# Keys and values of the last head loaded in two transfers each

## The chip, the cores and the metric

The kernel runs on one core of a Trainium2 chip. The metric is device time in microseconds (us), as the median of several executions; a profiled execution is recorded beside them, and all views below come from it. Within a core there are TensorE (PE, with its weight loads shown apart as PEld), VectorE (DVE), ScalarE (ACT), GpSimd (POOL) and SyncE (SP), and 16 DMA engines that move data between the device memory (HBM) and the core's memory (SBUF, 128 partitions). In this kernel SP issues nearly all DMAs, ACT four small ones at the start.

## The reference

One decode step (batch 1, one token, D = 576): a sigmoid gate mixes the output of an attention over the last W = 4096 cached keys with that of a dense GELU block.

```python
q = (x @ wq).reshape(1, 1, 32, 128).transpose(0, 2, 1, 3)
k = repeat(k_cache[:, :, Sk - W:, :], 2, axis=1)      # 16 key heads, Sk = 32768, W = 4096
v = repeat(v_cache[:, :, Sk - W:, :], 2, axis=1)
p = softmax(einsum("bhqd,bhkd->bhqk", q, k) * 128 ** -0.5)
a = einsum("bhqk,bhkd->bhqd", p, v).transpose(0, 2, 1, 3).reshape(1, 1, 4096) @ wo
b = gelu(x @ w1 + b1) @ w2 + b2                        # F = 4608
g = sigmoid((x * gate_w).sum(-1))
out = g * a + (1 - g) * b
```

Everything is bfloat16 in HBM. One head's keys are 4096 rows of 128 values, 1 MB; so are its values. With 16 heads that is 32 MB, and the four weight matrices are another 20 MB. A softmax followed by a weighted sum does not depend on the order of the keys, as long as keys and values are ordered alike.

## The kernel before

Each head's window of 4096 keys lies in one tile of 128 partitions x 32 chunks x 128 values. `load_k` (L83) and `load_v` (L90) fill it with one DMA: partition p gets the 32 consecutive rows 32p to 32p + 31, which is one run of 8 KB for each partition. `load_flat` (L99) loads pieces of `wq` and `w1` in the same way, one run for each partition (9,216 bytes, the last `w1` piece 4,608). `wo` (L421) has two runs of 4,608 bytes for each partition, `w2` (L431) one run of 10,368 bytes, its last group cut in two pieces of 6,912 and 3,456 bytes.

The instruction order is written by hand (`manual_schedule`, L72). The main loop (L395) runs over `h` from 0 to 20: it issues the keys of head h + 1 and the values of head h - 4, and, at five places, a piece of `w1`; then for each of eight groups of four chunks it transposes keys of head h + 1 on PE (`transposes`, L179: PE to PSUM, then DVE or ACT to SBUF), computes scores of head h (`scores`, L202), and multiplies values of head h - 5 (`values`, L265). Softmax runs for four heads at a time. After the loop SP issues four loads of `wo` and five of `w2` (L418 to L432), the last thing that the kernel reads. PE multiplies the attention output by `wo` (into `a_ps`) and the GELU output by `w2` (into `b_ps`, L496); one DVE instruction (L501) mixes both, and one DMA (L504) writes the output, four rows of 144.

So the order on SP's queue near the change is: values of head 9 and keys of head 15 (h = 14), values of heads 10 to 15, `wo` four times, `w2` five times, output. SP waits before an issue for two things where they apply: for a free buffer (10 for keys and values together, 8 for weights), and for the transfer issued eight places earlier, since the completion semaphores of its DMAs are used in turn, eight in all.

Four small loads go through ACT (L112 to L114): `x9` and `gw9` with 128 rows each, `b1g` with 4 rows of 2,304 bytes, `b2_row` with a single row of 1,152 bytes.

Of the kernel before, what the change touches and what calls it, by code (L numbers as in the profile page):

```python
# [9 lines left out]
BF16 = mybir.dt.bfloat16  # L10
# [6 lines left out]
def kernel(  # L17
# [15 lines left out]
    nc = tc.nc  # L33

    P = 128
    D = 576
    Hq, Hkv, Dh = 32, 16, 128
    Sk, W = 32768, 4096
    NCH = W // P
# [22 lines left out]
    kv_pool = ctx.enter_context(tc.tile_pool(name="kv_pool", bufs=10))  # L62
# [17 lines left out]
    NOG = Hq // OJ  # L80
    wo_view = A_wo.rearrange("(o p j) n -> p o (j n)", p=P, j=OJ)

    def load_k(h):  # L83
        t = kv_pool.tile([P, NCH, Dh], BF16, name="k_t", tag="kv")
        nc.sync.dma_start(  # L85
            out=t[:], in_=A_k_cache[0, h, Sk - W : Sk, :].rearrange("(p c) d -> p c d", p=P)
        )
        return t

    def load_v(h):  # L90
        t = kv_pool.tile([P, NCH, Dh], BF16, name="v_t", tag="kv")
        nc.sync.dma_start(  # L92
            out=t[:], in_=A_v_cache[0, h, Sk - W : Sk, :].rearrange("(p c) d -> p c d", p=P)
        )
        return t

    WMAX = RJ * D

# [15 lines left out]
    nc.scalar.dma_start(out=b2_row[:], in_=B_b2.rearrange("(o n) -> o n", o=1))  # L114

    k_tiles[0] = load_k(0)
    wq_t = []
    QP = NM * QB // 4
    for i in range(4):
        if i == 2:  # L120
            k_tiles[1] = load_k(1)
        wq_t.append(load_flat(wq_flat, i * QP * Dh, QP * Dh, "wq_t"))
# [15 lines left out]
    for o in range(2):  # L138
        nc.vector.tensor_reduce(
            out=par[:, o : o + 1],  # L140
            in_=ident_f[:].rearrange("p (i o) -> p o i", o=2)[:, o, :],
# [7 lines left out]
        out=turn[:].rearrange("p j (h q) -> p j h q", h=OJ),  # L149
        in_=ident[:].rearrange("p (o q j) -> p j o q", o=1, j=OJ).to_broadcast(  # L150
            [P, OJ, OJ, P // OJ]
        ),
# [4 lines left out]
        out=m_r[:], in_=ident_f[:].rearrange("p (s r) -> p r s", r=R), axis=AX.X, op=ALU.add  # L157
# [3 lines left out]
        out=m_hl[:], in_=ident_f[:].rearrange("p (h q) -> p h q", h=OJ), axis=AX.X, op=ALU.add  # L161
# [117 lines left out]
    for i in range(NBL):  # L279
# [5 lines left out]
        out=junk9[:], in0=x9[:], in1=gw9[:], scale=1.0, scalar=0.0,  # L285
# [11 lines left out]
        out=omg[:], in0=g_t[:], scalar1=-1.0, scalar2=1.0, op0=ALU.mult, op1=ALU.add  # L297
# [3 lines left out]
    for b in range(NM * QB):  # L301
# [3 lines left out]
        m, c = b // QB, b % QB  # L305
# [12 lines left out]
    for g in (1, 3):  # L318
        for hl in range(HB):
            lo = R * g + 2 * hl  # L320
            nc.vector.tensor_copy(  # L321
                out=qz[:, hl::HB, lo : lo + 2],
                in_=q_ps[:].rearrange("p o (b r) -> p (o b) r", r=R)[:, :, 2 * hl : 2 * hl + 2],
# [71 lines left out]
    for h in range(Hkv + LAG):  # L395
        if 1 <= h < Hkv - 1:
            k_tiles[h + 1] = load_k(h + 1)
        if 0 <= h - HB < Hkv:
            v_tiles[h - HB] = load_v(h - HB)
        w1_next = (W1_AT[h], w1_load(W1_AT[h])) if h in W1_AT else None  # L400
        for i in range(NBL):
            if 1 <= h < Hkv - 1:
                transposes(h + 1, i)
            if i in (2, 5) and h < Hkv:
                scores(h, i // 3)
            if i in (0, 1, 3, 6) and chain:
                chain.pop(0)()
            if h >= LAG:
                values(h - LAG, i)
        if w1_ready is not None:  # L410
            w1_mul(*w1_ready)
            if w1_ready[0] == len(PIECES) - 1:
                gelu()
        w1_ready = w1_next
        if h % HB == HB - 1 and h < Hkv:
            chain = softmax(h // HB)

    wo_t = []  # L418
    for i in range(NOG // 2):
        t = w_pool.tile([P, WMAX], BF16, name="wo_t", tag="w")  # L420
        nc.sync.dma_start(  # L421
            out=t[:, 0 : 2 * OJ * D].rearrange("p (o n) -> p o n", o=2),
            in_=wo_view[:, 2 * i : 2 * i + 2, :],
# [3 lines left out]
    for g in range(NG):  # L427
        t = w_pool.tile([P, WMAX], BF16, name="w2_t", tag="w")
# [8 lines left out]
        out=sg[:],  # L437
# [14 lines left out]
    for j in range(OJ):  # L452
# [3 lines left out]
        out=ow_m[:],  # L456
# [6 lines left out]
        out=ow_f[:].rearrange("p j o -> p (j o)"), in_=ow_m[:], axis=AX.X, op=ALU.add  # L463
# [17 lines left out]
    for o in range(NOG):  # L481
# [8 lines left out]
        out=a_sb[:], in0=a_ps[:], scalar1=g_t[:, 0:1], scalar2=None, op0=ALU.mult  # L490
# [5 lines left out]
    for g in range(NG):  # L496
# [5 lines left out]
        out=y[:], in0=b_ps[:], scalar=omg[:, 0:1], in1=a_sb[:], op0=ALU.mult, op1=ALU.add  # L502
    )
    nc.sync.dma_start(  # L504
        out=out.rearrange("a b (t n) -> (a b t) n", t=NQ), in_=y[0 : 32 * (NQ - 1) + 1 : 32, :]
# [31 lines left out]
```

## Time and profile before

| what | value |
|---|---|
| median of 3 executions | 138.4 us (138.38 to 138.7) |
| profiled execution, its time | 138.9 us |
| profiled execution, its span | 137.1 us |
| bytes moved by DMA | 53.88 MB in 8035 packets |
| PE, PEld, DVE, ACT busy | 75%, 61%, 42%, 31% of the span |
| granted TensorE clock, mean | 0.755 |
| transfer of 1 MB of keys, issue to landing | 20.0 us |

The span runs from the first to the last instruction; times on it are counted from its start. The execution's own time is 1.8 us longer than the span, for what lies around it. A DMA's "landing" is the moment at which all its parts have been reported complete. The trace also holds a record of every DMA packet (queue, bytes, start, duration), without the number of the engine that moved it, and of every increment of a semaphore.

### The profile page before, as it was taken

To read this page: it belongs to the slowest core of one execution; us is meant where nothing else is said; L and a number is where in the kernel's file an instruction comes from. 1 tells how busy PE (TensorE), PEld (TensorE's weight loads), DVE (VectorE), ACT (ScalarE), POOL (GpSimd) and SP (SyncE) were. 2 spreads that over 40 slices of the span, in tenths; PEclk is the share of its full clock that TensorE was granted. 3 is DMA by queue.
4 is the path that set the end of the run, shared out by engine and by line. 5 is a ranking of instruction groups with operands and counts; after the bars stand their busy time and mean duration, and the time that the engine had idled before them with its cause. 6 is when DMAs were issued, how large, how long until landed. Compare 5 with 4: busy or idle time off the path is not lost.

```text
span 137.1 us, 3928 instructions
## 1 busy us (share of the span) xinstructions
PE 103.5 (75%) x1779; PEld 83.4 (61%) x1779; DVE 57.4 (42%) x127; ACT 42.1 (31%) x75; POOL 1.4 (1%) x7
## 2 busy tenths in 40 slices
PE   0377765999969999988999986999795966343361
PEld 0357753768847977776877964788564855233350
DVE  5171431464477257735566367275723121010001
ACT  0351330355356246633356261554322000000000
POOL 4000000000000000000000000000000000000000
PEclk9999997579779779997589996589655555555555
DMA  4899999999999999999999999999999999999820
GB/s 153 350 418 422 423 427 426 425 427 428 421 421 421 422 415 418 418 418 423 426 419 416 423 415 417 421 413 421 421 421 419 417 418 421 432 430 421 359 105 8
DMA packets 8035, 53.88 MB, mean 393 GB/s; under 512 B 1101, under 2 KB 1102, under 8 KB 2514
## 3 DMA queue, kind: packets, MB, share of 16 engines
q1 hardware_dynamic: 7720, 53.61, 94.0%
q8 instruction: 14, 0.23, 0.7%
q10 hardware_dynamic: 298, 0.02, 0.1%
q14 instruction: 3, 0.02, 0.1%
HBM read 53.62 MB, written 0.00 MB: 391 GB/s over the span
## 4 chain that ended last, share of the span: by engine, by line
DMA 95%; SPq 1%; ACTq 0%; PE 0%; issue 0%; DVE 0%
DMA w_t<-in_B_w_dram 30%; DMA k_t<-in_A_k_cache_dram 29%; DMA wo_t<-in_A_wo_dram 16%; DMA v_t<-in_A_v_cache_dram 14%; DMA gw<-in_gate_w_dram 7%; SPq L85 1%; ACTq L112 0%; PE b_ps L471 0%; SPq L101 0%; DVE y L501 0%; SPq L92 0%
## 5 line engine op out<-in xcount | busy, mean ns | idle before, releaser
L184 PE MATMUL tp<-ident,k_t 128*128 128x128 bf16 x512 | 53.3, 255 | 10.0 <-DMA k_t<-in_A_k_cache_dram 8.2
L193 DVE CAST kT<-tp 128x512 bf16<-128x512 f32 x64 | 43.4, 689 | 33.8 <-PE tp L184 32.1
L195 ACT CAST kT<-tp 128x512 bf16<-128x512 f32 x64 | 37.5, 586 | 54.7 <-PE tp L184 54.3
L184 PEld LDWEIGHTS <-k_t 128*128 128x128 bf16 x512 | 38.0, 113 | 14.9 <-DMA k_t<-in_A_k_cache_dram 9.6
L270 PEld LDWEIGHTS <-v_t 128*128 128x128 bf16 x512 | 23.5, 105 | 7.3 <-issue 7.1
L270 PE MATMUL o_ps<-et,v_t 128*128 128x2 bf16 x512 | 26.8, 167 | 0.3 <-DVE et L259 0.3
L210 PE MATMUL s_ps<-kT,qz 128*32 128x512 bf16 x128 | 15.6, 486 | 0.7 <-DVE qz L321 0.7
L354 PE MATMUL h_ps<-x,w_t 128*128 128x2 bf16 x162 | 10.4, 199 | 0.0
L354 PEld LDWEIGHTS <-w_t 128*128 128x128 bf16 x162 | 10.1, 158 | 0.0
L471 PE MATMUL b_ps<-w_t,gt 128*1 128x144 bf16 x144 | 5.2, 320 | 5.7 <-DMA w_t<-in_B_w_dram 5.7
L471 PE MATMUL a_ps<-wo_t,ow 128*1 128x144 bf16 x128 | 4.5, 320 | 5.1 <-DMA wo_t<-in_A_wo_dram 4.0
L471 PEld LDWEIGHTS <-gt 128*1 128x1 bf16 x144 | 4.1, 115 | 6.7 <-issue 6.6
L471 PEld LDWEIGHTS <-ow 128*1 128x1 bf16 x128 | 3.6, 116 | 5.8 <-issue 4.6
L210 PEld LDWEIGHTS <-qz 128*32 128x32 bf16 x128 | 3.3, 96 | 4.6 <-issue 2.5
L307 PE MATMUL q_ps<-x,wq_t 128*128 128x2 bf16 x144 | 4.3, 166 | 2.2 <-DMA wq_t<-in_A_wq_dram 2.2
L307 PEld LDWEIGHTS <-wq_t 128*128 128x128 bf16 x144 | 4.2, 102 | 2.5 <-DMA wq_t<-in_A_wq_dram 2.5
L501 DVE SCALAR_TENSOR_TENSOR y<-b_ps,omg,a_sb 128x144 bf16<-128x144 f32 x1 | 0.4, 366 | 11.3 <-PE b_ps L471 11.3
L247 ACT ACTIVATE pr<-s_ps,nb 128x512 bf16<-128x512 f32 x4 | 2.7, 687 | 4.2 <-DVE nb L244 3.9
L489 DVE TENSOR_SCALAR a_sb<-a_ps,g_t 128x144 f32<-128x144 f32 x1 | 0.4, 367 | 8.6 <-PE a_ps L471 8.6
L232 PE MATMUL mT<-ident_f,mx 128*1 128x128 f32 x4 | 1.3, 321 | 3.4 <-DVE mx L228 3.4
L228 DVE TENSOR_REDUCE mx<-s_ps 128x1 f32<-128x512 f32 x4 | 2.7, 682 | 1.7 <-PE s_ps L210 1.7
L255 PE MATMUL pT<-ident,pr 128*128 128x128 bf16 x16 | 2.3, 289 | 0.7 <-ACT pr L247 0.7
(59 smaller groups left out, 26.8 us busy)
## 6 DMA issues: line engine op xcount, KB each, us to landing
k_t<-in_A_k_cache_dram SPq DMA_DIRECT2D x16, 1024.0 KB, 20.0
v_t<-in_A_v_cache_dram SPq DMA_DIRECT2D x16, 1024.0 KB, 20.3
wq_t<-in_A_wq_dram SPq DMA_DIRECT2D x4, 1152.0 KB, 12.4
w_t<-in_B_w_dram SPq DMA_DIRECT2D x4, 1152.0 KB, 20.4
wo_t<-in_A_wo_dram SPq DMA_DIRECT2D x4, 1152.0 KB, 21.0
w_t<-in_B_w_dram SPq DMA_DIRECT2D x3, 1296.0 KB, 21.2
w_t<-in_B_w_dram SPq DMA_DIRECT2D x1, 864.0 KB
w_t<-in_B_w_dram SPq DMA_DIRECT2D x1, 576.0 KB
```

The source lines that it names most:

```text
L85: nc.sync.dma_start(out=t[:], in_=A_k_cache[0, h, Sk - W : Sk, :].rearrange("(p c) d -> p c d", p=P))
L184: nc.tensor.matmul(tp[:, c * P : (c + 1) * P], lhsT=k_tiles[h][:, i * BC + c, :], rhs=ident[:], start=True, stop=True,)
L193: nc.vector.tensor_copy(out=dst, in_=tp[:])
L195: nc.scalar.copy(out=dst, in_=tp[:])
L210: nc.tensor.matmul(s_tiles[b][32 * t : 32 * (t + 1), :], lhsT=qz[:, h, lo : lo + 32], rhs=kT[h][:, i * BC * P : (i + 1) * BC * P], start=( ...
L228: nc.vector.tensor_reduce(out=mx[:], in_=s_ps[:], axis=AX.X, op=ALU.max)
L247: nc.scalar.activation(out=pr[:], in_=s_ps[:], func=ACT.Exp, bias=nb[:, 0:1], scale=SCALE, accum_out=sums[:, b : b + 1],)
L255: nc.tensor.transpose(out=pT[:, c, :], in_=pr[:, c * P : (c + 1) * P], identity=ident[:])
L270: nc.tensor.matmul(o_ps[:, 2 * h : 2 * h + 2], lhsT=v_tiles[h][:, i * BC + c, :], rhs=ets[b][:, c, col : col + 2], start=(i == 0 and c == ...
L307: nc.tensor.matmul(q_ps[:, :, c], lhsT=wq_t[b // QP][:, off : off + Dh], rhs=x2[:, m, :], start=(b == 0), stop=(m == NM - 1), skip_group_c ...
L354: nc.tensor.matmul(h_ps[:, j, gl::GH], lhsT=t[:, off : off + U - RJ + 1 : RJ], rhs=x2[:, m, :], start=False, stop=(m == NM - 1), skip_grou ...
L471: nc.tensor.matmul(acc[32 * t : 32 * t + 1, :], lhsT=col, rhs=rows[:, t * DQ : (t + 1) * DQ], start=start, stop=stop,)
```

## The change

`load_k` and `load_v` call a common `load_kv`. For heads 0 to 14 it issues the same DMA as before. For head 15 it issues two. The first fills chunks 0 to 23 of each partition from the first 3,072 rows of the window (partition p gets rows 24p to 24p + 23, a run of 6,144 bytes). The second fills chunks 24 to 31 from the last 1,024 rows, cut into 128 blocks of eight rows (2,048 bytes). Its source is written with three dimensions: 8 rows, 16 blocks in each, 2,048 bytes in a block; block number 8b + a goes to partition 16a + b. The destination is 128 partitions of 2,048 bytes. Which key sits in which partition and chunk changes for head 15, in the same way for keys and values.

```diff
+    CE = 8
+
+    def load_kv(cache, h, name):
+        t = kv_pool.tile([P, NCH, Dh], BF16, name=name, tag="kv")
+        src = cache[0, h, Sk - W : Sk, :]
+        if h < Hkv - 1:
+            nc.sync.dma_start(out=t[:], in_=src.rearrange("(p c) d -> p c d", p=P))
+            return t
+
+        CA = NCH - CE
+        nc.sync.dma_start(
+            out=t[:, 0:CA, :], in_=src[0 : P * CA, :].rearrange("(p c) d -> p c d", p=P)
+        )
+        nc.sync.dma_start(
+            out=t[:, CA:NCH, :],
+            in_=src[P * CA : W, :].rearrange("(b a c) d -> a b (c d)", a=8, b=P // 8),
+        )
+        return t
+
     def load_k(h):
-        t = kv_pool.tile([P, NCH, Dh], BF16, name="k_t", tag="kv")
-        nc.sync.dma_start(
-            out=t[:], in_=A_k_cache[0, h, Sk - W : Sk, :].rearrange("(p c) d -> p c d", p=P)
-        )
-        return t
+        return load_kv(A_k_cache, h, "k_t")
 
     def load_v(h):
-        t = kv_pool.tile([P, NCH, Dh], BF16, name="v_t", tag="kv")
-        nc.sync.dma_start(
-            out=t[:], in_=A_v_cache[0, h, Sk - W : Sk, :].rearrange("(p c) d -> p c d", p=P)
-        )
-        return t
+        return load_kv(A_v_cache, h, "v_t")
```

PE, DVE, ACT and POOL execute the same instructions in the same order as before; SP has two more DMA issues.

More of the change, by code (lines that the diff above doesn't have):

```diff
@@ L81, with load_k @@
     wo_view = A_wo.rearrange("(o p j) n -> p o (j n)", p=P, j=OJ)
-    def load_k(h):
-        t = kv_pool.tile([P, NCH, Dh], BF16, name="k_t", tag="kv")
-        nc.sync.dma_start(
-            out=t[:], in_=A_k_cache[0, h, Sk - W : Sk, :].rearrange("(p c) d -> p c d", p=P)
-        )
-        return t
+    CE = 8
[6 more added lines that the diff above has]
+        CA = NCH - CE
+        nc.sync.dma_start(
+            out=t[:, 0:CA, :], in_=src[0 : P * CA, :].rearrange("(p c) d -> p c d", p=P)
[3 more added lines that the diff above has]
+            in_=src[P * CA : W, :].rearrange("(b a c) d -> a b (c d)", a=8, b=P // 8),
+        )
+        return t
+    def load_k(h):
+        return load_kv(A_k_cache, h, "k_t")
     def load_v(h):
-        t = kv_pool.tile([P, NCH, Dh], BF16, name="v_t", tag="kv")
-        nc.sync.dma_start(
-            out=t[:], in_=A_v_cache[0, h, Sk - W : Sk, :].rearrange("(p c) d -> p c d", p=P)
-        )
-        return t
+        return load_kv(A_v_cache, h, "v_t")
     WMAX = RJ * D
```

## The prediction

> **What bounds the kernel now.** I read the chain of waits first. By engine it is nearly all DMA, and in order of time (start, us, what) it ends with a load of `w2`:
>
> ```profile
> DMA 95%; SPq 1%; ACTq 0%; PE 0%; issue 0%; DVE 0%
> ```
> ```profile
> 112.74 20.78 DMA w_t<-in_B_w_dram
> 133.52 0.04 issue
> 133.56 0.56 PE b_ps L471 x11
> 134.12 0.02 issue
> 134.15 0.37 DVE y L501
> ```
>
> The last transfer lands at 133.52; 3.6 us of matmuls, mix and output follow whatever came before. So the time is 133.52 plus a fixed tail, and only an earlier last landing helps. Next, the DMA rows of the page (40 slices of 3.43 us) and the DMA view of the stretch 126.0 to 137.1 alone (40 slices of 0.28 us):
>
> ```profile
> DMA  4899999999999999999999999999999999999820
> GB/s 153 350 418 422 423 427 426 425 427 428 421 421 421 422 415 418 418 418 423 426 419 416 423 415 417 421 413 421 421 421 419 417 418 421 432 430 421 359 105 8
> ```
> ```profile
> DMA  9998998999687665543322210000200000000100
> ```
>
> The 16 DMA engines run full from the second slice on at about 420 GB/s, yet they do not stop together: from 129 us on the busy share falls step by step until 133. Engines run out of work one after the other, and the last one sets the end.
>
> Why are they uneven? Every big load gives each engine the same bytes. The page's queues and the semaphore records tell:
>
> ```profile
> q1 hardware_dynamic: 7720, 53.61, 94.0%
> q8 instruction: 14, 0.23, 0.7%
> ```
>
> Queue 8 fetches instructions, 14 packets of 16 KB. On one engine a packet's record starts 4 ns before the previous one ends, within 1 ns nearly throughout, so the packet records can be chained into 16 engines. The chains show that the 14 fetches go round eight engines in turn and never touch the other eight. A fetch sets its engine back by about 1.5 us (a fetch at 90.9: the spread of one transfer's 16 increments was 2.60 us before it and 4.15 after). The last `w2` piece's 16 increments, from the semaphore records, on the span's scale:
>
> ```
> eight engines without a fetch: 129.35 129.37 129.54 129.72 130.14 130.44 130.47 130.69
> one fetch each:                131.49 131.51 131.91
> two fetches each:              132.60 132.75 133.11 133.24 133.52
> ```
>
> The two groups do not overlap. Call them early and late: the early group is done 2.83 us before the end (133.52 - 130.69).
>
> **The change part by part.** *How many engines the second transfer uses.* The semaphore records show an increment for each engine that took part: 16 for the loads with 128 rows, 4 for `b1g` with 4 rows, 1 for `b2_row` with one (both beside one more from the issuer, for the rest). A source of 8 rows onto 128 partitions is not in this trace; between 8 and 16 engines I take 8, since the rows cannot be dealt to 16 without cutting them. *Which eight.* Following the four `b1g` packets (from 8.84 to 9.13 us) along their chains, three end on early engines for certain; the fourth, which also carried `b2_row`, meets another chain at the same nanosecond at 15.7 us, and of the two continuations one is early and the other late (its small irregularities go on in the early one). So small row counts seem to use the same engines, nested, none of them where the fetches go; I take the eight to be the early group.
>
> [...]
>
> *Price of bytes.* Packet records by size, median: 4,608 bytes 178 ns, 8,192 bytes 309 ns. That is 131 ns for 3,584 bytes, so 2,048 bytes are worth 74.9 ns and a packet has 9.6 ns of its own, of which 4 overlap.
>
> *First transfers.* On each engine 8 packets of 8,192 become 8 of 6,144 bytes: 8 x 74.9 = 0.60 us less for each of keys and values, 1.20 us in all on every engine. For the late group that is the whole change: its last engine ends at 133.52 - 1.20 = 132.32.
>
> *Second transfers.* 128 blocks over 8 engines are 16 packets of 2,048 bytes each. No row has that size. By the line above a packet takes 84.5 - 4 = 80.5 ns from start to start; the nearest rows give bounds: `b2_row`'s 1,152 bytes took 73 ns (69 net), `b1g`'s 2,304 bytes 93 ns (89 net). I take 80.5 and add 5 ns for the completion write: 16 x 80.5 + 5 = 1.29 us, less the 0.60 saved, so +0.69 us for each transfer and +1.39 for both. The early group's last engine ends at 130.69 + 1.39 = 132.08 (bounds 131.71 and 132.35). It stays within 0.03 us of the late group's 132.32 at worst.
>
> *Sum.* The last landing goes from 133.52 to 132.32 (bounds 132.32 to 132.35): -1.20 us. In the profiled execution's own time 138.9 - 1.2 = 137.7; that execution stands 0.5 us above the median of 138.4, so the median becomes 137.2.
>
> *Issues on SP.* Two more, 0.33 us each by the rows of `k_t`, at most the 0.65 us of the output's issue:
>
> ```profile
> 52.18 0.33 SPq L85 DMA_DIRECT2D k_t<-in_A_k_cache_dram  x1
> 54.66 0.33 SPq L92 DMA_DIRECT2D v_t<-in_A_v_cache_dram  x1
> 57.16 0.33 SPq L85 DMA_DIRECT2D k_t<-in_A_k_cache_dram  x1
> ...
> 134.54 0.65 SPq L504 DMA_DIRECT2D out_dram<-y  x1
> ```
>
> Behind them wait the values of heads 10 to 15, `wo` and `w2`. Each issue waits for the transfer eight places before, so one more place delays each of them by about one step of 2.5 us (52.18, 54.66, 57.16). What hides this is the stock of work in the queue: 20.0 us from issue to landing for 1 MB. With two of the eight places filled by 0.75 and 0.25 MB the stock is 7 MB instead of 8, some 17.5 us; even the early engines, which run up to 4.2 us ahead, do not empty it. Cost nothing; without that cover, a step of 2.5 us.
>
> *PE.* The last two of eight groups of head 15 wait for the second transfer. It follows the first in the queue and rides the engines that are ahead, so these groups can wait a little longer for each other, but PE is only half busy from 110 us on (7.95 of 16 us between 110 and 126), and nothing on the path that ends last hangs on it. The order of keys changes in no instruction.
>
> [...] By the trace, 512 KB on eight engines costs these eight time and frees the others of it. [...] Were all engines in step, that would make the end 1.39 us later by the prices above (139.8 us); the falling busy share before the end says that they are not.
>
> **The rivals.**
>
> *A. The eight engines are, or include, the late ones.* For it: only three of four are sure, and nothing shows four of the early eight under a small load. Against: fetches turn over exactly eight engines, and those three are not among them. The carriers pay +1.39 us, so the kernel ends at 133.52 + 1.39 = 134.91: 139.8 us, slower. It decides as soon as any carrier ended after 132.13 before (133.52 - 1.39), which are the five engines with two fetches. [...]
>
> *B. All 16 engines share the second transfer*, split by the 128 partitions. For it: `x9`, whose source has 64 rows, landed by 16. Against: the same count for 64 and 128 says nothing of 8. Each engine then has 8 packets of 8,192 as 16 of 6,144 and 2,048: for both loads 2 x (8 x 5.6 + 5) = 0.10 us more: 138.5 us, no change.
>
> *C. Blocks of 2,048 bytes, 16 KB apart on one engine, are much slower than 89 ns.* For it: no row has such a step, and 1,152 bytes were dear at 73 ns. Against: `b1g`'s 93 ns came at full load. At 110 ns net the early group ends at 130.69 + 2 x (1.76 + 0.005 - 0.60) = 133.02: 137.9 us. From 126 ns on (130.69 + 2.83) it is slower than before.
>
> **How the numbers follow.** Forecast (two groups, eight early carriers) 0.70; A 0.10; B 0.07; C 0.13, of which faster 0.08, no change 0.02, slower 0.03. A change under 0.3%, 0.4 us, cannot be told from none here. Faster 0.70 + 0.08 = 0.78; same 0.07 + 0.02 = 0.09; slower 0.10 + 0.03 = 0.13. The time is the forecast's 137.2. The medians shown differ by up to 0.3 us, which sets the low end, 136.9; upward the range takes in most of C and B, to 138.5, and leaves out A and the dear part of C. The forecast's own range is 136.9 to 137.5.
>
> **What would show it right or wrong.** Right: 256 packets of 2,048 bytes at 80 to 90 ns; 8 increments and one of the issuer for each second transfer; the last `w2` piece's increments within about 2 us of each other instead of 4.2, two groups ending near 132.1 and 132.3; last landing 1.2 us earlier, same 14 fetches. Wrong: 16 increments (B); spread grown to about 6.8 us (A); packets over 100 ns (C); gaps on the DMA engines before 126 us, if the queue's stock did run out.

## The result, and the profile after

The changed kernel is slower: a median of 143.0 us (141.35 to 143.3, four executions) against 138.39 us, a ratio of 1.0305 with a 95% interval of 1.0265 to 1.0345. The profiled execution took 143.3 us, its span is 141.5 us; before it was 138.9 and 137.1. So 4.4 us of span are to be found. Ratios, here and below, compare the means of executions in the fast state; one execution of `e1_near` below, of 142.87 us, is left out of its ratio as a slow one.

The end of the chain of waits, in order of time (start, us, what), is the same as before, only later: the last piece of `w2` lands at 137.91 instead of 133.52, and the tail behind it is unchanged.

```profile
115.52 22.38 DMA w_t<-in_B_w_dram
137.91 0.04 issue
137.95 0.56 PE b_ps L482 x12
138.50 0.02 issue
138.53 0.37 DVE y L512
```

The page's DMA rows of the changed kernel (40 slices of 3.54 us) show where it was lost:

```profile
DMA  4999999999999999999999999999999999999710
GB/s 137 372 405 421 416 423 428 427 423 424 419 421 426 414 419 417 419 424 421 424 419 421 421 406 422 367 289 419 419 417 349 300 414 424 432 430 420 317 58 3
```

There are two dips in GB/s, at 88 to 95 us and at 106 to 113, while the busy digits stay at 9: the DMA engines were not short of work, their packets took longer. These are the stretches in which the two second transfers ran. The view by stretches gives (stretch and its length, busy us of PE, PEld, DVE, ACT, POOL with counts, granted TensorE clock, DMA share, GB/s), first for the kernel before, then for the changed one:

```profile
90.00:96.00 6.00, 5.70 (x112) 4.90 (x108) 3.49 (x10) 3.19 (x7) 0.00 (x0) 0.97 1.01 418
96.00:107.00 11.00, 8.64 (x134) 6.43 (x132) 4.80 (x12) 3.02 (x6) 0.00 (x0) 0.56 1.01 418
107.00:113.00 6.00, 4.58 (x136) 4.23 (x133) 1.29 (x6) 0.00 (x0) 0.00 (x0) 0.50 1.02 416
```
```profile
90.00:96.00 6.00, 6.00 (x112) 5.34 (x110) 3.70 (x6) 2.93 (x5) 0.00 (x0) 0.87 1.04 315
96.00:107.00 11.00, 8.77 (x142) 6.53 (x140) 5.45 (x15) 2.72 (x6) 0.00 (x0) 0.61 1.01 416
107.00:113.00 6.00, 4.15 (x133) 4.01 (x133) 0.52 (x2) 0.52 (x2) 0.00 (x0) 0.50 1.03 309
```

Between the dips the rate is the old one (416 against 418). In the dips it is 315 and 309 instead of 418 and 416: 103/418 x 6 us + 107/416 x 6 us = 3.0 us lost by all 16 engines together.

The packet records say whose packets grew. The 256 packets of 2,048 bytes had a median of 131 ns (the first ones 84). Summed over all packets from 15 us on, the time above each size's undisturbed record, divided by 16 engines and less the same sum before, is 0.71 us for 2,048 bytes, 0.58 for 6,144 (the first transfers), 0.69 for 8,192 (other keys and values) and 1.09 for the 4,608 bytes of `wo`. More than three quarters of the loss fell on packets other than those of the second transfers.

The 16 increments of the last `w2` piece, on the span's scale, summed up:

```
                mean of the 16    last    last - mean
before               131.24      133.52      2.28
changed              134.67      137.91      3.24
```

The mean moved by 3.4 us, about what the dips cost (engines were 0.26 us later in the mean already at 32 us), and the last engine stands another 1.0 us further behind the mean than before. Two questions follow: why the packets were slow, and which engines were loaded.

### The profile page after: what moved, and what is told of

Read it like the earlier page. It is cut to its first block, busy times and chain, and to the rows that moved or that the text cites. A ratio compares the mean times of both kernels' runs of the same rounds, so it can differ in the third digit from the quotient of the medians.

```text
span 141.5 us, 3930 instructions
## 1 busy us (share of the span) xinstructions
PE 102.4 (72%) x1779; PEld 82.9 (59%) x1779; DVE 57.5 (41%) x127; ACT 41.9 (30%) x75; POOL 1.4 (1%) x7
## 4 chain that ended last, share of the span: by engine, by line
DMA 90%; PE 5%; DVE 1%; SPq 1%; ACTq 0%; issue 0%; DVEq 0%
DMA k_t<-in_A_k_cache_dram 40%; DMA w_t<-in_B_w_dram 16%; DMA v_t<-in_A_v_cache_dram 14%; DMA wo_t<-in_A_wo_dram 14%; DMA gw<-in_gate_w_dram 6%; PE tp L195 2%; PE h_ps L365 2%; DVE kT L204 1%; ACTq L123 0%; PE h_ps L353 0%; PE b_ps L482 0%; SPq L112 0%; DVE y L512 0%; SPq L89 0%; PE s_ps L221 0%
## 5 line engine op out<-in xcount | busy, mean ns | idle before, releaser
L281 PEld LDWEIGHTS <-v_t 128*128 128x128 bf16 x512 | 24.0, 106 | 8.5 <-issue 7.3
```

What stands on the lines that cost most here:

```text
L281: nc.tensor.matmul(o_ps[:, 2 * h : 2 * h + 2], lhsT=v_tiles[h][:, i * BC + c, :], rhs=ets[b][:, c, col : col + 2], start=(i == 0 and c == ...
```

## The experiments

Each ratio below is to the kernel before on the same chip, whose median was 138.46 or 138.47 us throughout. The theories are named as in the expectations: S, the step between the blocks in HBM makes them slow; N, eight engines instead of sixteen are the cost; P, the place in SBUF, partitions that other engines write at the same time. No trace here names the engine or the partition of a packet. That one engine carries one row of a source is my reading of the increments (eight for the 8 rows of each second transfer in the changed kernel, four for `b1g` with 4 rows and one for `b2_row` with one row before), which partitions a row fills follows from the kernel's text, and which engines fill them in the 128-row loads is P's assumption.

**The source without its step** (`e1_near`), in the changed kernel:

```diff
-            in_=src[P * CA : W, :].rearrange("(b a c) d -> a b (c d)", a=8, b=P // 8),
+            in_=src[W - 1152 : W, :].rearrange("(a r) d -> a r d", a=8)[:, 0 : P, :].rearrange(
+                "a (b c) d -> a b (c d)", c=CE
+            ),
```

> The second transfer keeps 8 rows of 16 blocks of 2,048 bytes and the same destination, but the 16 blocks of a row are neighbours in HBM (32 KB in one piece) instead of 16 KB apart. It reads 1,024 of the last 1,152 rows of the window, so 128 keys come twice and 128 are left out, and the output differs for that. Theory S (the step in the source makes the blocks slow): packets of 2,048 bytes fall from the changed kernel's 131 ns to 84 to 90 ns, no dip of the DMA rate, time 137.2 to 139.8 us depending on which engines carry them. Theory P (the eight engines write partitions that other engines are writing at the same time): nothing changes, packets about 130 ns, time 141.5 to 143.3 us.

Measured 141.24 us, ratio 1.0187 (1.0147 to 1.0226). The packets kept a median of 128.5 ns, and the two dips are there, 276 and 275 GB/s in the worst of 40 slices of 3.48 us:

```profile
GB/s 134 396 403 428 420 428 423 429 426 424 421 416 423 425 410 423 416 419 417 430 423 414 423 412 423 409 276 385 416 423 402 275 405 422 422 431 420 404 171 3
```

S is out as the cause of the slow packets. The time is 1.8 us below the changed kernel's, though, and just below the 141.5 us that P expected at the least; "Which engines" comes back to it.

**The same cut over 128 rows** (`e2_step`): both transfers take column pieces of the old layout.

```diff
-            out=t[:, 0:CA, :], in_=src[0 : P * CA, :].rearrange("(p c) d -> p c d", p=P)
+            out=t[:, 0:CA, :], in_=src.rearrange("(p c) d -> p c d", p=P)[:, 0:CA, :]
...
-            in_=src[P * CA : W, :].rearrange("(b a c) d -> a b (c d)", a=8, b=P // 8),
+            in_=src.rearrange("(p c) d -> p c d", p=P)[:, CA:NCH, :],
```

> Two transfers each, but the second with 128 source rows of 2,048 bytes (the last eight chunks of each partition's old run, 8 KB apart), so all 16 engines share it as they share every other load. Theory S (small blocks with a step in the source are slow): packets of 2,048 bytes above 100 ns, time 139 to 141 us. Theory P (the place written to): packets 84 to 90 ns, no dip of the rate, 138.4 to 138.7 us. The same 138.4 to 138.7 us from theory N (using eight engines alone is the cost).

Measured 138.65 us, ratio 1.0011 (0.9998 to 1.0024). The 256 packets took 84 to 91 ns (5% to 95%). Splitting the load, two more issues and blocks of 2,048 bytes cost nothing that can be told. The same three stretches of this run have the old rates:

```profile
90.00:96.00 6.00, 6.00 (x112) 5.34 (x111) 3.74 (x7) 2.92 (x5) 0.00 (x0) 0.87 1.02 416
96.00:107.00 11.00, 8.14 (x142) 6.36 (x140) 5.40 (x15) 3.24 (x7) 0.00 (x0) 0.77 1.01 415
107.00:113.00 6.00, 4.79 (x145) 4.51 (x143) 1.25 (x5) 0.00 (x0) 0.00 (x0) 0.50 1.03 418
```

**Four transfers of 32 partitions** in place of the one second transfer (`e3_four`), and **16 rows of 8 blocks** (`e4_rows16`):

```diff
+        for m in range(4):
+            lo = P * CA + 256 * m
+            nc.sync.dma_start(
+                out=t[32 * m : 32 * (m + 1), CA:NCH, :],
+                in_=src[lo : lo + 256, :].rearrange("(b a c) d -> a b (c d)", a=8, b=4),
+            )
```
```diff
-            in_=src[P * CA : W, :].rearrange("(b a c) d -> a b (c d)", a=8, b=P // 8),
+            in_=src[P * CA : W, :].rearrange("(b a c) d -> a b (c d)", a=16, b=P // 16),
```

> The second transfer is cut into four of 32 partitions each, each with a source of 8 rows of 4 blocks 16 KB apart: still eight engines, still 2,048-byte blocks, but engine a now writes partitions 4a to 4a + 3 of the 32. Theory P: the eight engines no longer meet each other, and only two of the four quarters meet another engine's normal partitions; 2,048-byte packets fall in two groups, near 84 to 90 ns and above 110 ns; excess packet time well below the changed kernel's 1.6 us an engine and transfer; 138.5 to 141 us. Theory S or N: all packets stay near 130 ns, 141.5 to 143.5 us.

> The second transfer has a source of 16 rows of 8 blocks (32 KB apart) instead of 8 rows of 16: all 16 engines take part, engine a writing partitions 8a to 8a + 7. Theory N (eight engines alone is the cost): 138.4 to 138.7 us, packets 84 to 90 ns. Theory S (step in the source): packets 120 ns or more. Theory P: packets 100 to 140 ns where engines meet, half as many of them an engine, excess below 0.8 us an engine and transfer, 138.6 to 140.2 us.

`e3_four`: 140.86 us, 1.0178 (1.0155 to 1.02). The packets came in two kinds, as P has it: of the keys' 128 packets in order of time, the first four eighths (the first pair of quarters) have medians of 84, 84, 86 and 106 ns, the last four 166, 133, 102 and 116 ns. The excess fell less than I had said: the dips remain (300 and 274 GB/s).

`e4_rows16`: 141.28 us, 1.0206 (1.0187 to 1.0225), a median of 105 ns, and slower than the 140.2 us that P allowed. All 16 engines took part, the dips are there, and the loss is as large as in `e1_near` with eight:

```profile
90.00:96.00 6.00, 4.88 (x98) 4.04 (x96) 3.98 (x12) 2.75 (x6) 0.00 (x0) 1.00 1.02 337
96.00:107.00 11.00, 9.15 (x152) 6.96 (x152) 4.37 (x10) 2.94 (x6) 0.00 (x0) 0.51 1.01 415
107.00:113.00 6.00, 3.98 (x116) 3.62 (x113) 0.01 (x1) 0.00 (x0) 0.00 (x0) 0.50 1.02 336
```

So N is out as the cause of the dips: what `e2_step` and `e4_rows16` do not share is the shape of the source, and with it, by the reading above, who writes which partition (and the step in HBM, which the next runs settle).

**The place alone.** The kernel before, unchanged, with extra transfers behind the last keys and the last values into a spare tile that nothing reads. `f1_low` is below; `f2_high` differs in one number, the first partition (64 + 32 * m):

```diff
+        if h == Hkv - 1:
+            x = const.tile([P, 8 * Dh], BF16, name="x_" + name)
+            for m in (0, 1):
+                nc.sync.dma_start(
+                    out=x[32 * m : 32 * (m + 1), :],
+                    in_=src[256 * m : 256 * (m + 1), :].rearrange("(b a c) d -> a b (c d)", a=8, b=4),
+                )
```

`f3_eights` sends the same bytes to partitions 0 to 63 in one transfer (a=8, b=8), `f4_stride` 128 rows with the changed kernel's 16 KB step to all partitions:

```diff
...
+                out=x[:],
+                in_=cache[0, h, Sk - 2 * W : Sk, :].rearrange("(p c) d -> p c d", p=P)[:, 0:8, :]
+                .rearrange("p c d -> p (c d)"),
...
```

> The kernel before, whose last keys and values are each followed by two extra transfers of 64 KB into a spare tile that nothing reads: sources of 8 rows of 4 blocks of 2,048 bytes, 16 KB apart, onto partitions 0 to 31 and 32 to 63, so that each of eight engines writes four partitions. Theory P (a transfer is slow where its engines write partitions that other engines write in the normal loads; by the earlier quarters these partitions are the engines' own): 2,048-byte packets 84 to 90 ns, excess packet time below 0.1 us, no dip of the rate; the eight engines get 2 x 8 x 80 ns = 1.3 us more, so 138.4 us if none of them is a late one, up to 139.8 us if one is. Theory S (step or form of the source): packets 100 ns or more, as in the next run.

> As the run with partitions 0 to 63, same sources, bytes, engines and number of transfers, but onto partitions 64 to 95 and 96 to 127. Theory P: these are other engines' partitions; packets 120 ns or more, packets of other transfers beside them lengthened too, excess 0.4 to 0.8 us an engine for each pair, time 139.3 to 141 us. Theory S: no difference from the run before.

> The same extra bytes onto partitions 0 to 63, but in one transfer of 8 rows of 8 blocks, so engine a writes partitions 8a to 8a + 7 instead of four of its own in each half. Theory P: the engines meet each other and each other's normal loads; packets 100 to 140 ns, excess 0.3 to 0.8 us a transfer, 139 to 140.5 us. Theory S: as the run onto partitions 0 to 63 in quarters.

> The kernel before with one extra transfer of 256 KB after the last keys and one after the last values into a spare tile: 128 source rows of 2,048 bytes, 16 KB apart as in the changed kernel, over all 16 engines and their normal partitions. Theory P: packets 84 to 90 ns, excess below 0.1 us, time longer by the bytes alone, 2 x 8 x 80 ns = 1.3 us: 139.7 us. Theory S: packets above 100 ns and 140.3 us or more.

```
run          us      ratio (95%)                2,048-byte packets, 5% / median / 95%, ns
f1_low     139.85   1.0094 (1.0074 to 1.0113)      84 /  84 /  85
f2_high    141.54   1.0218 (1.0195 to 1.0241)      84 / 117 / 177
f3_eights  142.01   1.0223 (1.0162 to 1.0284)      84 / 104 / 160
f4_stride  139.94   1.0107 (1.0081 to 1.0133)      84 /  84 /  88
```

The stretches of `f1_low`, then of `f2_high`:

```profile
90.00:96.00 6.00, 4.47 (x81) 4.06 (x80) 3.83 (x11) 2.09 (x5) 0.00 (x0) 0.83 1.01 415
96.00:107.00 11.00, 9.15 (x142) 6.62 (x140) 3.94 (x10) 3.02 (x6) 0.00 (x0) 0.50 1.01 419
107.00:113.00 6.00, 4.28 (x133) 3.98 (x130) 1.15 (x5) 0.00 (x0) 0.00 (x0) 0.50 1.01 413
```
```profile
90.00:96.00 6.00, 3.07 (x62) 2.66 (x60) 2.97 (x10) 1.99 (x4) 0.00 (x0) 0.83 1.01 325
96.00:107.00 11.00, 9.29 (x151) 7.21 (x151) 4.40 (x9) 3.12 (x6) 0.00 (x0) 0.66 1.02 422
107.00:113.00 6.00, 3.51 (x126) 3.43 (x126) 0.24 (x2) 0.00 (x0) 0.00 (x0) 0.50 1.01 320
```

Same bytes, sources, engine count and number of transfers; moved by 64 partitions, the rate falls from 415 to 325 and from 413 to 320 GB/s. `f4_stride` cost 1.48 us, where its bytes were estimated at 2 x 8 x 80 ns = 1.3 us, and its packets took 84 ns: the 16 KB step did not slow them. Nor are the high partitions slow as such: `e2_step` and `f4_stride` write all 128 at 84 ns, and `f3_eights`, which deals the low 64 out differently, is slow on them. P is shown as far as it goes: the partitions decide (84 ns in `f1_low`, 117 in `f2_high`), and on the same partitions how they are dealt to the rows (104 in `f3_eights`). That the packets are slow where an engine writes partitions that other engines write in the 128-row loads agrees with both, but is my reading; no run shows why. Its sizes were too small: `f2_high` and `f3_eights` are slower than the 141 and 140.5 us that P allowed.

**Which engines.** `f1_low` has no slow packets, so its records can be chained, and the engines that carry 2,048-byte packets stand out: six without a fetch, and two that had two fetches. The last `w2` completions were written by those two, at 133.78 and 133.96, the next engine at 132.97 (starts of packet records; the increments are recorded some 0.45 us later). To see it from the load, longer blocks, and four engines instead of eight:

```diff
-            x = const.tile([P, 8 * Dh], BF16, name="x_" + name)
+            x = const.tile([P, 28 * Dh], BF16, name="x_" + name)
...
-                    in_=src[256 * m : 256 * (m + 1), :].rearrange("(b a c) d -> a b (c d)", a=8, b=4),
+                    in_=src[896 * m : 896 * (m + 1), :].rearrange("(b a c) d -> a b (c d)", a=8, b=4),
```

`g2_four` and `g3_four_long` have a=4 and the partitions 0 to 15 and 32 to 47, with blocks of 2,048 and 7,168 bytes.

> The kernel before with extra transfers onto partitions 0 to 63 as in the cheap run above (eight engines, partitions of their own), but with blocks of 7,168 bytes: 16 packets of about 268 ns, 4.3 us more on each of the eight engines, nothing on the others. If all eight are early engines (end 130.7 at the latest), the last landing goes from 133.5 to 135.0 and the time to 139.9 us. If late engines are among them: 133.5 + 4.3, 142.7 us.

> Extra transfers of 4 rows of 4 blocks of 2,048 bytes onto partitions 0 to 15 and 32 to 47: four engines only, 1.3 us more on each. If these four are early engines (as the chains of the four-row bias load said), nothing changes: 138.4 to 138.6 us. If a late engine is among them: up to 139.8 us.

> As the run on four engines, with blocks of 7,168 bytes: 4.3 us more on each of the four. If they are early: their last end 130.7 at most becomes 135.0, time at most 139.9 us. If a late one is among them: 142.7 us.

`g2_four`: 138.61 us, 1.0016 (1.0002 to 1.003): 1.3 us more on four engines are nearly free. `g3_four_long`: 140.92 us, 1.0173 (1.0149 to 1.0196), 1 us above what I allowed for four early engines and 1.8 below the other case; in its profiled execution (140.59, the lowest of four) the four carriers are the four last, at 133.44 to 134.64 by their packet records, none with a fetch, and the last landing is 135.10, near the expected 135.0. Half of the microsecond is my own slip: I set the landings of an execution of 138.9 us against the median of 138.46. The rest was not followed. These four engines are early.

`g1_eight_long`: 141.67 us, 1.0253 (1.019 to 1.0317), between the two cases. Two of its 16 last increments, at 129.98 and 130.14, are of engines that were early and carried nothing, and the last, 136.04, is a microsecond beyond what eight early carriers could reach by the landings of the kernel before: the eight are not the early group. Its records, chained in the same way, show six carriers without a fetch and two, the last to end, with one fetch each. Engines with one fetch ended at 131.49 to 131.91 before, and 4.3 us more is 135.8 to 136.2. So two of the eight engines of such a load served fetches in these two runs, but how many fetches these two have had differs from run to run: two each in `f1_low`, one each here.

The same explains most of the difference between `e1_near` and the changed kernel, as far as one trace of each can. The changed kernel's two last increments, 137.58 and 137.91, stand two microseconds behind the next, 135.62, and followed back they are of the engines that served the fetches at 119.1 and 128.8, the twelfth and thirteenth, so of engines with two. In `e1_near` the engines of the twelfth and thirteenth fetch (118.5 and 127.0) end among the others. The mean of the last increments there is 134.14, half a microsecond earlier than in the changed kernel, but the last is only 1.53 us behind the mean instead of 3.24. That the two last engines were carriers is read from their distance; the chains could not be followed through the dips.

**Half of the change** (`h1_keys`):

```diff
-        if h < Hkv - 1:
+        if h < Hkv - 1 or name == "v_t":
```

> The changed kernel with only the last head's keys loaded in two transfers; its values come as before, in the old order, so the last head's weights meet the values of other keys. Theory P with two late engines among the eight: one dip instead of two, excess 1.5 to 1.7 us an engine instead of 3.2, half of the loss: 140.3 to 141.2 us. If the loss hung on the second pair alone (the values' transfers, nearer to the end), 138.4 to 138.8 us; if on the first alone, 142 us or more.

Measured 139.88 us, 1.0113 (1.0079 to 1.0148): a loss of 1.4 us, less than half of 4.6 and below my range. There is one dip. The trace is of the fastest of six executions (139.19; the slowest took 140.74), and in it the last landing is only 0.39 us later than before, 133.91. The mean of the last increments moved by 1.44 us (131.24 to 132.68), as one dip should, but the last engine is 1.23 us behind that mean instead of 2.28. The four last increments, 133.70 to 133.91, are of engines with two fetches, none apart from the others, so here too no engine with two fetches seems to have carried the second transfer. The changed kernel's trace is of the slowest of its four executions, and there two such engines are last. So the halves are unequal in these two traces at least in part because other engines were last, and not only because the second pair is dearer; what each half costs on average was not separated.

## Why the prediction was wrong

Right: the last landing sets the time and the tail behind it did not move; 256 packets of 2,048 bytes; eight engines (the semaphores of the two second transfers show nine increments, eight and one of the issuer); 14 instruction fetches; the cover for the issues held: SP issued the second transfers in 0.77 and 0.63 us (the first above the 0.65 that I allowed), and the engines had work throughout.

```profile
74.68 0.33 SPq L93 DMA_DIRECT2D k_t<-in_A_k_cache_dram  x1
77.11 0.77 SPq L96 DMA_DIRECT2D k_t<-in_A_k_cache_dram  x1
...
93.72 0.63 SPq L96 DMA_DIRECT2D v_t<-in_A_v_cache_dram  x1
```

Wrong, first: the step *Second transfers*. "By the line above a packet takes 84.5 - 4 = 80.5 ns", with bounds of 69 and 89, is about what a packet of this size takes in the places of `e2_step`, `f1_low` and `f4_stride` (records of 84 ns, so 80 net). Here it took 131 ns. The bounds came from rows of small loads whose place I did not look at; I bounded size and never asked which partitions a row of 16 blocks puts in one engine's hands. Rival C named the symptom and its turning point, 126 ns, but gave the step in HBM as the reason, and that reason fell in `e1_near` and `f4_stride`. A smaller slip: the median of the 8,192-byte packets is 311 ns, 309 is only their most frequent value; with 311 the price is 79.0 ns instead of 80.5, and the sum changes by less than 0.1 us.

Wrong, second, and larger: the sum held that an engine outside the eight gains 1.20 us. I had no term for what a transfer does to others' packets, and that is more than three quarters of the 3.0 us lost in the dips. Slow packets on the carriers alone are not enough: at 131 ns rival C's sum puts the early group's end at 133.69, 0.2 us later than before, where 137.91 was measured. `f2_high` against `f1_low` prices the place at 1.7 us for 256 KB in all.

Wrong, third: *Which eight*. "I take the eight to be the early group" rested on three certain chains of four engines. The four are early (`g2_four`), the step to eight was a guess: two of the eight were late ones, with two fetches each in `f1_low` and one each in `g1_eight_long`. `f1_low`, free of slow packets, cost 1.39 us, about the 1.3 us of bytes added to the engine that ends last. So rival A was right on this part, and the gain of 1.2 us was out of reach even at 84 ns a packet. By the prediction's own prices (+0.69 us a transfer on a carrier) a kernel without slow packets would have lost 1.39 us, rival A's 139.8, where the two late carriers have two fetches each; where they have one, it would have ended at 131.91 + 1.39 = 133.30, 0.2 us earlier than before. That kernel was not run: the places that cost nothing in `f1_low` are 64 of the 128 partitions.

Confining the transfers to eight engines, the argument against the change that the prediction weighed, covers only the smaller part, the 1.4 us of `f1_low`: `e4_rows16` has 16 rows outermost, uses all engines, and still loses 2.8 us.

No version here beats the kernel before. The early engines' spare time is real (`g2_four`), but in every run here with slow packets or a dip of the rate the loss, from 1.4 us (`h1_keys`) to 4.6 us (the changed kernel), was larger than any gain.

## What to carry to other kernels

In these runs the shape of a DMA's source decided how many engines shared it (16 increments for 128 rows, eight for 8) and, by my reading, which partitions each of them wrote. The same extra bytes left the rate of all loads together at 415 GB/s when they went to one half of the partitions, and at 325 when they went to the other (`f1_low`, `f2_high`). Price a new shape by the packets it disturbs, not only by its own, and test it as an extra transfer into a spare tile. An uneven finish of the DMA engines is worth reading from the last load's 16 increments, but know which engines a small load uses before building on it.

## What the runs showed of the hardware

By the packet chains of the kernel before, the 14 instruction fetches of 16 KB fell on the same eight of 16 engines in turn and set an engine back by about 1.5 us each (the spread of one transfer's increments went from 2.60 to 4.15 us with the fetch at 90.9). The last load's increments ended 4.17 us apart there, those of the eight engines without a fetch within 1.34 us. Two of the eight engines that carried the 8-row loads of `f1_low` and of `g1_eight_long` had fetches, two each in the one and one each in the other; six had none. And a second transfer of 256 KB, 8 rows of 16 blocks, cost all 16 engines of the changed kernel some 1.5 us (3.0 us for two, at 315 and 309 GB/s instead of 418 and 416), on top of the 256 KB / 420 GB/s = 0.6 us that its bytes alone take at the page's rate. How it comes to be so large was not settled.
